# Fourier mixing and MLP layers: the last product with w4 as seven block products, channels by tokens, behind all of w3

## The chip, the core and the metric

The kernel runs on one core of a Trainium2 chip. TensorE multiplies, VectorE (DVE) and ScalarE (ACT) do the elementwise work, GpSimd (POOL) a few small ones, and SyncE (SP) issues every DMA from one queue, in order. The metric is the time of one execution in microseconds on the device. Before the change three executions took 1460.28, 1461.61 and 1462.27 us; the median is 1461.61 us.

## The reference

The input x has 2048 tokens of 512 channels in float32. Two layers A are interleaved with two layers B, each added to its input:

```python
x = x + A(layernorm(x)); x = x + B(layernorm(x)); x = x + A(layernorm(x)); x = x + B(layernorm(x))
def A(x):   # Fourier mixing, real part
    a = x @ dft_hid_re.T; b = x @ dft_hid_im.T
    return dft_seq_re @ a - dft_seq_im @ b
def B(x):   # w1, w2: 512x512, w3: 512x1376, w4: 1376x512
    h = gelu(layernorm(x) @ w1)            # then each quarter of h is shifted by -2..+2 tokens
    x1 = x + shifted(h) @ w2
    return x1 + gelu(layernorm(x1) @ w3) @ w4
```

## The kernel before

Every matrix operand is split into a high and a low part, and `mm3` (L283 to L286) makes each product from three matmuls of a 128x128 stationary block with 512 moving columns: high by high, high by low, low by high. The split of an operand is one ACT cast (the high part) and one DVE subtraction (the low part). The hidden width 1376 is padded to NF = 11 blocks of 128. The tokens are cut into four chunks of 512 (c = 0 to 3), each of four tiles of 128.

**Order.** There is no planner: each engine runs its instructions in the order of the code, and waits where an operand is not ready or a buffer is not yet free. That holds for SP too, so a DMA that waits holds up all DMAs behind it.

**The first layer's B.** `by_pairs` (L766) does w1 and w2 for all four chunks, and then w3 and w4 for chunks 0 and 1 together. w3 is done by seven block products in place of eight (a scheme of Winograd's kind: columns of the two chunks, halves of the channels and pairs of hidden blocks), from sums of w3's blocks that DVE makes, splits, and also stores to DRAM (`w3_sums`, `w3_lows`, `w3_keep`, L882 to L906) for the second layer. w4 is done plainly by `w4_part` (L1012): tokens by channels, 12 matmuls per hidden block and chunk. Chunks 2 and 3 then go one after the other through `mlp` (L712) in STEPS = 13 steps t: step t multiplies w3's block t (12 matmuls, gelu on ACT, split on DVE) and, from t = 2, the hidden block t - 2 by w4 (12 matmuls). `stream` (L272) hands each step its weights from a ring of four buffers: at step t it issues the DVE subtraction for step t + 2's weights (L247), the load of a raw buffer behind it (L212), and the ACT cast of step t + 3's (L230). From step 7 of chunk 2 on, the code after `mlp`'s yield (L1335 to L1353) also puts in the preparation of the second layer's first stage, on DVE and ACT.

**The second layer's B.** `by_pairs` runs two pairs. In each, a loop over p (five of them) does the seven block products for two hidden blocks of both chunks (42 matmuls), and between them two `w4_part`s for the first chunk; the second chunk's gelus are kept in `hc`, and its eleven `w4_part`s follow behind the loop, without a break, as the last work of the kernel. The rows of `out` are stored as tokens by channels.

Of the kernel before, what the change touches and what calls it, by code (L numbers as in the profile page):

```python
# [8 lines left out]
F32 = mybir.dt.float32  # L9
F32R = mybir.dt.float32r  # L10
AF = mybir.ActivationFunctionType
# [29 lines left out]


@with_exitstack
def spectral_mlp_kernel(ctx: ExitStack, tc: tile.TileContext, x, ws, hs, w1, w2, w34, out):
    nc = tc.nc
    const = ctx.enter_context(tc.tile_pool(name="const", bufs=1))
    small = ctx.enter_context(tc.tile_pool(name="small", bufs=4))
# [14 lines left out]
    w3d = [dram.tile([P, 2, 7, 2 * P], F32, name=f"w3d{i}") for i in range(NF // 2)]  # L62
    w3e = dram.tile([P, 2, CH], F32, name="w3e")
    w4d = [dram.tile([P, 2, CH], F32, name=f"w4d{i}") for i in range(NF)]

# [52 lines left out]
    scratch = [at(f"scr{i}", RNG + w * 4 * CH, KD, CH, dtype=F32) for i, w in enumerate((2, 3, 0))]  # L118
    extra = [at(f"extra{i}", EXT + i * D, D, dtype=F32) for i in range(6)]
    rest = [at(f"rest{i}", RAWS + i * D, D, dtype=F32) for i in range(8)]  # L120

    def xt(j):
        return xs[j // 2][:, j % 2]
# [156 lines left out]
        return slots.pop(i)  # L280


    def mm3(o, lh, ll, rh, rl, first, last):  # L283
        nc.tensor.matmul(o, lh, rh, start=first, stop=False)  # L284
        nc.tensor.matmul(o, lh, rl, start=False, stop=False)  # L285
        nc.tensor.matmul(o, ll, rh, start=False, stop=last)  # L286

    def stats(srcs):

# [158 lines left out]
    def add(o, a, b, op=ALU.add):  # L448
        nc.vector.tensor_tensor(o, a, b, op=op)
# [196 lines left out]
    def split_low(dst, g):  # L646
        nc.vector.tensor_tensor(dst[:, 1], g, dst[:, 0].bitcast(F32), op=ALU.subtract)
# [110 lines left out]
    def prod(o, w, u, b):  # L758
        for d in range(2):
            v = slice(d * P, (d + 1) * P)  # L760
            mm3(o, w[:, 0, u, v], w[:, 1, u, v], blk[b][:, d, 0], blk[b][:, d, 1], d == 0, d == 1)

    def rt_in(c):
        nc.sync.dma_start(rtf[c % 2][:, :, 1], z3d[c].rearrange("(d p) t -> p d t", p=P))

    def by_pairs(layer, zs, xin, dst):  # L766
        act = nc.scalar.copy
        w1p = [stream(), stream()]
# [74 lines left out]
        fs = [NF - 1] + list(range(NF - 1))  # L843
        order = [None] + fs + fs
        n_pairs = 1 if layer == 0 else NC // 2
        seq, used = {"n": 0}, {"n": 0}

        def w4_fresh(n):
# [1 line left out]

        def w4_load():
            n = seq["n"]
            if n == n_pairs * len(order):
# [176 lines left out]
        def one():  # L1030
            if bg:
                bg.pop(0)()

        for pair in range(n_pairs):
            c1, c2 = 2 * pair, 2 * pair + 1
            bk, acc1 = (mm4, acc4) if pair == 0 else (acc4, mm4)
            acc2 = [bk[(1 + i) % 4] for i in range(4)]
# [140 lines left out]
    for layer in range(LAYERS):  # L1178
# [153 lines left out]
            break  # L1332

        tmps[:] = singles
        for c in (2, 3):  # L1335
            for t in mlp(c, acc4, mm4):
                if c == 2 and t == 1:
                    rt_in(3)
                if c == 2 and t in (9, 10):
                    rt_split(3, ((2 * t - 18, 2 * t - 16),))  # L1340
                if c == 3 and t == 1:
                    for j in range(2 * TC, 3 * TC, 2):
                        rows(xs[j // 2], x2d, j, 2, False)
# [63 lines left out]
```

## Time and profile before

| what | value |
|---|---|
| median of three executions | 1461.61 us |
| span of the profiled execution, first to last instruction | 1459.5 us |
| median less the span of the profiled execution | 2.1 us |
| TensorE busy | 1450.2 us, 99% of the span |
| DVE, ACT busy | 1123.6 us (77%), 717.9 us (49%) |
| chunks 2 and 3 of the first layer (`mlp`) | from 618.4 us |
| last pair of the second layer | from 1341.4 us |

The profiled execution has no time of its own beside its span; the median above stands for it, 2.1 us longer than the span. In the views, L12 is line 12 of the kernel; names such as psd or w3b are tiles with their numbers left out, "out<-in" tells what an instruction writes and reads, and the text in brackets how long its engine sat idle before it and what ended that. "SPq" is SP's DMA queue; a DMA row gives the issue alone, and "to landing" the time from issue until the data is there. TensorE rows overlap: the time one matmul costs is the distance between two starts, not the duration in the row.

### The profile page before, as it was taken

Reading aid. Unit: us, or ns where it says so; the run is one execution under the profiler, and the core shown is the slowest. Engines: PE = TensorE matmul, PEld = TensorE weight load, DVE = VectorE, ACT = ScalarE, POOL = GpSimd, SP = SyncE. Lnnn points to the kernel's source line nnn. Section 1 sums busy time; section 2 is a strip of 40 time slices with the busy share of each in tenths; the row PEclk is TensorE's granted clock in tenths of the full one; section 3 lists DMA queues with packets and bytes.
Section 4 is the critical chain, followed back from the end, with each engine's and each line's share of the span. In section 5 each row is a group of like instructions: output and inputs, shape, how many; then the busy total and the mean of one; then the engine's idle time right before and its main releaser. Section 6 shows DMA issues by size and latency. Waiting matters only on the chain.

```text
span 1459.5 us, 17324 instructions
## 1 busy us (share of the span) xinstructions
PE 1450.2 (99%) x6374; PEld 1189.0 (81%) x6374; DVE 1123.6 (77%) x1560; ACT 717.9 (49%) x953; POOL 86.4 (6%) x111
## 2 busy tenths in 40 slices
PE   9999999999999999999999999999999999999998
PEld 7888888888878788887887888888887788888887
DVE  7876987988868896658889978979797788646443
ACT  5563454444556664335554543545445575423231
POOL 2100000000001000001100000000000010000000
PEclk9999999999999999999999999999999999999999
DMA  7336556556545767842445555564665466768434
GB/s 251 124 95 209 192 187 212 188 186 235 185 136 169 237 237 278 264 150 86 139 137 195 169 199 204 165 230 173 209 229 168 130 173 260 236 225 295 157 126 159
DMA packets 110500, 277.17 MB, mean 190 GB/s; under 512 B 8400, under 2 KB 37072, under 8 KB 108496
## 3 DMA queue, kind: packets, MB, share of 16 engines
q1 hardware_dynamic: 110416, 276.07, 56.5%
q8 instruction: 50, 0.82, 0.2%
q14 instruction: 34, 0.28, 0.1%
HBM read 231.21 MB, written 44.83 MB: 189 GB/s over the span
## 4 chain that ended last, share of the span: by engine, by line
PE 86%; DVE 8%; DMA 3%; issue 1%; ACT 1%; SPq 0%; POOL 0%; DVEq 0%; ACTq 0%; POOLq 0%
PE psd L284 9%; PE psd L286 9%; PE psd L285 9%; PE psa L284 8%; PE psa L286 7%; PE psa L285 7%; PE psc L286 6%; PE psc L284 6%; PE psc L285 6%; PE psb L286 6%; PE psb L284 6%; PE psb L285 6%; DVE ring L247 2%; DMA raw<-in_ws 2%; DVE ring3f L236 0%
## 5 line engine op out<-in xcount | busy, mean ns | idle before, releaser
L230 ACT CAST ring<-raw 128x1024 fp32r<-128x1024 f32 (+1 forms) x153 | 156.9, 1031 | 122.8 <-PE psd L286 49.3
L247 DVE TENSOR_TENSOR ring<-raw,ring 128x1024 fp32r<-128x1024 f32 (+1 forms) x154 | 182.1, 1186 | 28.6 <-ACT ring L230 28.5
L286 PE MATMUL psd<-ring,rr 128*128 128x512 f32 x208 | 80.9, 389 | 0.0
L285 PE MATMUL psd<-ring,rr 128*128 128x512 f32 x208 | 80.9, 389 | 0.0
L284 PE MATMUL psd<-ring,rr 128*128 128x512 f32 x208 | 80.9, 389 | 0.0
L324 POOL TENSOR_TENSOR rs<-ve,mhalf 128x4 f32<-128x4 f32 x16 | 27.8, 1739 | 612.9 <-DVE nm L323 612.9
L303 POOL TENSOR_TENSOR rs<-ve,mhalf 128x2 f32<-128x2 f32 (+1 forms) x33 | 32.9, 998 | 405.8 <-DVE nb L302 405.8
L332 ACT ACTIVATE tmp<-xs,nb,rs 128x512 f32<-128x512 f32 x58 | 44.7, 810 | 16.3 <-POOL nb L304 16.3
L237 ACT CAST ring<-ring2f 128x1024 fp32r<-128x1024 f32 x28 | 29.6, 1057 | 44.2 <-DVE ring2f L236 44.2
L285 PE MATMUL psc<-ring,ay 128*128 128x512 f32 x128 | 50.0, 391 | 1.0 <-DVE ring L247 1.0
L284 PE MATMUL psc<-ring,ay 128*128 128x512 f32 x128 | 49.9, 390 | 0.3 <-ACT rr11f L474 0.3
L237 ACT CAST ring<-ring0f 128x1024 fp32r<-128x1024 f32 x28 | 29.6, 1058 | 41.5 <-DVE ring0f L236 41.5
L286 PE MATMUL psc<-ring,ay 128*128 128x512 f32 x128 | 49.9, 390 | 0.0
L284 PE MATMUL psb<-ring,ay 128*128 128x512 f32 x128 | 49.8, 389 | 0.0
L285 PE MATMUL psb<-ring,ay 128*128 128x512 f32 x128 | 49.8, 389 | 0.0
L286 PE MATMUL psb<-ring,ay 128*128 128x512 f32 x128 | 49.8, 389 | 0.0
L247 DVE TENSOR_TENSOR ring<-ring1f,ring 128x1024 fp32r<-128x1024 f32 (+1 forms) x50 | 49.2, 984 | 0.6 <-ACT ring L233 0.4
L247 DVE TENSOR_TENSOR ring<-ring3f,ring 128x1024 fp32r<-128x1024 f32 (+1 forms) x50 | 49.2, 984 | 0.2
L284 PE MATMUL psd<-ring,ay 128*128 128x512 f32 x126 | 49.0, 389 | 0.0
L286 PE MATMUL psd<-ring,ay 128*128 128x512 f32 x126 | 49.0, 389 | 0.0
L284 PE MATMUL psa<-ring,ay 128*128 128x512 f32 x126 | 49.0, 389 | 0.0
L285 PE MATMUL psa<-ring,ay 128*128 128x512 f32 x126 | 49.0, 389 | 0.0
(481 smaller groups left out, 4353.4 us busy)
## 6 DMA issues: line engine op xcount, KB each, us to landing
raw<-in_ws SPq DMA_DIRECT2D x183, 512.0 KB, 4.9
raw<-in_hs SPq DMA_DIRECT2D x56, 512.0 KB, 3.5
w4r<-w4d SPq DMA_DIRECT2D x55, 512.0 KB, 3.8
w3b<-w3d SPq DMA_DIRECT2D x10, 1792.0 KB, 7.5
raw<-in_w SPq DMA_DIRECT2D x26, 512.0 KB, 3.7
w3d<-w3b SPq DMA_DIRECT2D x5, 1792.0 KB, 6.7
x1d<-tmp SPq DMA_DIRECT2D x12, 512.0 KB, 6.8
xs<-x1d SPq DMA_DIRECT2D x12, 512.0 KB, 6.7
```

The costliest lines, as they stand in the source:

```text
L230: nc.scalar.copy(dest[:, a:b, 0], r[0][:, a:b])
L237: nc.scalar.copy(dest[:, :, 0], lo)
L247: nc.vector.tensor_tensor(lo[:, i], src[:, i], hi[:, i].bitcast(F32), op=ALU.subtract)
L284: nc.tensor.matmul(o, lh, rh, start=first, stop=False)
L285: nc.tensor.matmul(o, lh, rl, start=False, stop=False)
L286: nc.tensor.matmul(o, ll, rh, start=False, stop=last)
L303: nc.gpsimd.tensor_tensor(rs[:, :n], ve[:, :n], mhalf[:, 0, :n], op=ALU.pow)
L324: nc.gpsimd.tensor_tensor(rs, ve, mhalf[:, :, :2], op=ALU.pow)
L332: nc.scalar.activation(o, s, AF.Identity, bias=mr[2], scale=mr[1])
```

## The change

Only the second layer's last pair (chunks 2 and 3) and the place where its weights come from are changed.

- **Last pair.** `last_pair` does all of w3 first: the leftover block's 24 matmuls, and then five rounds of 42, now with eight PSUM banks in turn. All gelus (22 blocks of 128x512) stay in SBUF, and DVE makes 21 sums of them (t1, t2, t3 in place of b12, t4 in place of b21). Then w4 is done the other way round, channels by tokens: weights are the stationary operand and hidden blocks the moving one. Seven passes of 30 matmuls (five steps of six) do ten hidden blocks; 24 matmuls for the eleventh are spread over passes 0, 1, 3 and 4. Every step's hidden block is split by an ACT cast and a DVE subtraction three steps ahead (`split_of`). The last pass's matmuls are issued only at its end, first all for one bank, then all for the other.
- **Weights.** Each pass loads its five blocks, 1,310,720 bytes in rows of 1 KB, from `w4s` in DRAM into one of two buffers, which lie where w3's two buffers were. The load for pass i + 1 is issued as pass i begins.
- **First layer.** w4's sums and splits are made in steps 0 to 7 of chunk 2's `mlp`, right behind each step's own instructions: `w4_ahead(t)` stores pair t - 2 of hidden blocks to `w4s` (1792 KB), makes pair t - 1's low parts on DVE, makes pair t's sums on DVE (four of 128x256) and its casts on ACT, and loads pair t + 1 (512 KB). The sums of pair t go into the buffer from which pair t - 2 is stored, since there are two.
- **Result.** Chunks 2 and 3 leave as `out_t`, channels by tokens, in their natural order; the residual is transposed in 32x32 blocks on DVE, stored and loaded again. The host turns `out_t` back.

```diff
--- before.py
+++ after.py
...
@@ -62,6 +62,9 @@
     w3d = [dram.tile([P, 2, 7, 2 * P], F32, name=f"w3d{i}") for i in range(NF // 2)]
     w3e = dram.tile([P, 2, CH], F32, name="w3e")
     w4d = [dram.tile([P, 2, CH], F32, name=f"w4d{i}") for i in range(NF)]
+    w4s = dram.tile([P, NF // 2, 2, 7, 2 * P], F32, name="w4s")
+    w4e = dram.tile([P, 2, 4, 2 * P], F32, name="w4e")
+    resd = [dram.tile([D, CH], F32, name=f"resd{i}") for i in range(2)]
...
@@ -118,6 +121,19 @@
     scratch = [at(f"scr{i}", RNG + w * 4 * CH, KD, CH, dtype=F32) for i, w in enumerate((2, 3, 0))]
     extra = [at(f"extra{i}", EXT + i * D, D, dtype=F32) for i in range(6)]
     rest = [at(f"rest{i}", RAWS + i * D, D, dtype=F32) for i in range(8)]
+    w4c, w4cf = zip(*(both(f"w4c{i}", word, 2, 7, 2 * P) for i, word in enumerate((W12, 0))))
+    w4raw = [at(f"w4raw{i}", word, 2, CH, dtype=F32) for i, word in enumerate((STG, EXT, EXT + 2 * CH))]
...
+    h_at = [XS + i * CH for i in range(4)] + [W12 + i * CH for i in range(NF + 4)]
+    h_at += [ZW + i * CH for i in range(8)] + [RR + (8 + i) * CH for i in range(8)]
+    hq = [at(f"hq{i}", word, CH, dtype=F32) for i, word in enumerate(h_at)]
+    hs_at = [XS + 4 * CH, XS + 6 * CH, STG] + [H3 + 2 * i * CH for i in range(4)] + [XS + 12 * CH, XS + 14 * CH]
+    hsplit = [at(f"hs{i}", word, 2, CH) for i, word in enumerate(hs_at)]
+    w4u = [at(f"w4u{i}", RNG + 8 * CH + i * 28 * P, NF // 2, 2, 2 * P) for i in range(2)]
+    w4t = at("w4t", XS + 8 * CH, 2, 4, 2 * P)
...
@@ -763,6 +779,58 @@
     def rt_in(c):
         nc.sync.dma_start(rtf[c % 2][:, :, 1], z3d[c].rearrange("(d p) t -> p d t", p=P))
+    W4_UNITS = {"12": 0, "1": 1, "2": 2, "3": 3, "a11": 4, "a12": 5, "a22": 6}
...
+    def w4_raw(n):
+        to = w4raw[n % 3]
+        if n < NF // 2:
+            nc.sync.dma_start(to, w34[2 * n + LAG : 2 * n + LAG + 2, :, 1].rearrange("f p w -> p f w"))
+        else:
+            nc.sync.dma_start(to[:, 0], w34[NF - 1 + LAG, :, 1])
+    def w4_parts(n):
+        r, lo = w4raw[n % 3].rearrange("p f (e w) -> p f e w", e=2), w4cf[n % 2][:, 1]
+        if n < NF // 2:
+            return [(slice(0, 4), lo[:, 0:4]), (slice(4, 6), r[:, :, 0]), (slice(6, 7), r[:, 1, 1:2])]
+        return [(slice(0, 2), lo[:, 0:2]), (slice(2, 4), r[:, 0])]
+    def w4_sums(n):
+        lo = w4cf[n % 2][:, 1]
+        (a11, a21), (a12, a22) = ([w4raw[n % 3][:, f, e * 2 * P : (e + 1) * 2 * P] for e in range(2)] for f in range(2))
+        if n < NF // 2:
+            add(lo[:, 1], a21, a22)
+            add(lo[:, 3], a11, a21, ALU.subtract)
+            add(lo[:, 2], lo[:, 1], a11, ALU.subtract)
+            add(lo[:, 0], a12, lo[:, 2], ALU.subtract)
+        else:
+            add(lo[:, 0], a11, a21, ALU.subtract)
+            add(lo[:, 1], a21, a11, ALU.subtract)
+        for units, src in reversed(w4_parts(n)):
+            nc.scalar.copy(w4c[n % 2][:, 0, units], src)
+    def w4_lows(n):
+        w = w4c[n % 2]
+        for units, src in reversed(w4_parts(n)):
+            nc.vector.tensor_tensor(w[:, 1, units], src, w[:, 0, units].bitcast(F32), op=ALU.subtract)
+    def w4_keep(n):
+        w = w4c[n % 2].bitcast(F32)
+        if n < NF // 2:
+            nc.sync.dma_start(w4s[:, n], w)
+        else:
+            nc.sync.dma_start(w4e, w[:, :, 0:4])
+    def w4_ahead(t):
+        if 0 <= t - 2 <= NF // 2:
+            w4_keep(t - 2)
+        if 0 <= t - 1 <= NF // 2:
+            w4_lows(t - 1)
+        if 0 <= t <= NF // 2:
+            w4_sums(t)
+        if t + 1 <= NF // 2:
+            w4_raw(t + 1)
...
@@ -850,7 +919,7 @@
         def w4_load():
...
+        def last_pair():
...
+            def split_of(m):
+                key, b = steps[m][2], hsplit[m % len(hsplit)]
+                if key[0] == "t4":
+                    q = key[1]
+                    add(slots["b21", q], slots["t2", q], slots["b21", q], ALU.subtract)
+                    slots[key] = slots["b21", q]
+                nc.scalar.copy(b[:, 0], slots[key])
+                split_low(b, slots[key])
+                splits[m] = b
+            def gelu_to(key, src):
+                nc.scalar.activation(slot(key), src, AF.Gelu_apprx_tanh)
+            def residual(c):
+                return [
+                    *[lambda q=q: [turn_one(turn4, i, xt(c * TC + i)) for i in (q, q + 1)] for q in (0, 2)],
+                    lambda: turn_out(turn4, resd[c - c1]),
+                ]
+            def res_in(i):
...
+            def sums(p):
+                t1 = slot(("t1", p))
+                add(t1, slots["b12", p], slots["b11", p], ALU.subtract)
+                if p < NF // 2:
+                    t2 = slot(("t2", p))
+                    add(t2, slots["b22", p], t1, ALU.subtract)
+                    add(slots["b12", p], slots["b22", p], slots["b12", p], ALU.subtract)
+            todo = residual(c1) + [lambda: None] * 4 + residual(c2)
...
+            def w4_in(i, u):
+                nc.sync.dma_start(w4u[i % 2].bitcast(F32), w4s[:, :, :, W4_UNITS[u]])
+            last = NF // 2
+            passes = [
+                ("a11", "b11", 2), ("2", "t2", 0), ("a12", "b21", None), ("1", "t1", 3),
+                ("3", "b12", 1), ("12", "b22", None), ("a22", "t4", None),
+            ]
+            steps = []
+            for i, (u, h, e) in enumerate(passes):
+                steps += [(i, p, (h, p), None) for p in range(NF // 2)]
+                if e is not None:
+                    steps.append((i, last, ("t1" if h == "t2" else h, last), e))
+            for p in range(NF // 2):
+                u, v, x, y = sets[p % 2]
+                w = w3b[(5 + p) % 2]
+                b1, b6, b5, b2, b7, b4, b3 = (bank() for _ in range(7))
...
+                sums(p - 1 if p else last)
...
+                if p == last - 1:
+                    w4_in(0, passes[0][0])
+                    split_of(0)
+                    split_of(1)
...
+                w3_load(5 + p + 2)
+                if p == 3:
+                    nc.sync.dma_start(w4t.bitcast(F32), w4e)
+            assert not todo
+            w4_in(1, passes[1][0])
+            for i in range(2):
+                res_in(i)
+            c_1, y_12 = part4[:2]
...
+            def give(i, half, src, bk, op=ALU.add, which=(0, 1)):
+                r = resid[i][:, 2 * half : 2 * half + 2]
+                for j in which:
+                    add(r[:, j], src[:, j], bk[j], op)
+                    nc.sync.dma_start(out_v[:, 2 * half + j, i * CH : (i + 1) * CH], r[:, j])
+            def after(i, bk):
+                if i == 0:
+                    for j in range(2):
+                        nc.scalar.copy(c_1[:, j], bk[j])
+                    sums(last - 1)
+                if i == 1:
+                    for j in range(2):
+                        add(c_1[:, j], c_1[:, j], bk[j])
+                if i == 2:
+                    give(0, 0, resid[0][:, 0:2], bk)
+                if i == 3:
+                    for j in range(2):
+                        add(y_12[:, j], c_1[:, j], bk[j])
+                    for half in range(2):
+                        r = resid[1][:, 2 * half : 2 * half + 2]
+                        add(r, r, y_12)
+                if i == 4:
+                    give(1, 1, resid[1][:, 2:4], bk)
+                    for j in range(2):
+                        add(c_1[:, j], c_1[:, j], bk[j])
+                    add(resid[0][:, 2:4], resid[0][:, 2:4], c_1)
+                if i == 5:
+                    give(1, 0, resid[1][:, 0:2], bk)
+            bks, kept = {}, []
+            for k, (i, p, key, e) in enumerate(steps):
+                if k + 3 < len(steps):
+                    split_of(k + 3)
+                first = p == 0
+                if first:
+                    bks[i] = bks[0] if i == 2 else [bank(), bank()]
+                    if 0 < i < len(passes) - 1:
+                        w4_in(i + 1, passes[i + 1][0])
+                w = w4u[i % 2][:, p] if e is None else w4t[:, :, e]
+                h = splits.pop(k)
+                end = k + 1 == len(steps) or steps[k + 1][0] != i
+                if i == len(passes) - 1:
+                    kept.append((w, h))
+                    continue
+                for j in range(2):
+                    v = slice(j * P, (j + 1) * P)
+                    mm3(bks[i][j], w[:, 0, v], w[:, 1, v], h[:, 0], h[:, 1], first and i != 2, end, i == 2)
+                if end:
+                    after(i, bks[i])
+            for j in range(2):
+                v = slice(j * P, (j + 1) * P)
+                for p, (w, h) in enumerate(kept):
+                    mm3(bks[i][j], w[:, 0, v], w[:, 1, v], h[:, 0], h[:, 1], p == 0, p == last - 1)
+                give(0, 1, resid[0][:, 2:4], bks[i], ALU.subtract, (j,))
         for pair in range(n_pairs):
+            if pair:
+                last_pair()
+                break
             c1, c2 = 2 * pair, 2 * pair + 1
             bk, acc1 = (mm4, acc4) if pair == 0 else (acc4, mm4)
             acc2 = [bk[(1 + i) % 4] for i in range(4)]
@@ -1332,8 +1579,11 @@
             break
         tmps[:] = singles
+        w4_raw(0)
         for c in (2, 3):
             for t in mlp(c, acc4, mm4):
+                if c == 2:
+                    w4_ahead(t)
                 if c == 2 and t == 1:
                     rt_in(3)
                 if c == 2 and t in (9, 10):
...
```

More of the change, by code (lines that the diff above doesn't have):

```diff
@@ L43, in spectral_mlp_kernel @@
 @with_exitstack
-def spectral_mlp_kernel(ctx: ExitStack, tc: tile.TileContext, x, ws, hs, w1, w2, w34, out):
+def spectral_mlp_kernel(ctx: ExitStack, tc: tile.TileContext, x, ws, hs, w1, w2, w34, out, out_t):
     nc = tc.nc
@@ L120, in spectral_mlp_kernel @@
     rest = [at(f"rest{i}", RAWS + i * D, D, dtype=F32) for i in range(8)]
+    w4c, w4cf = zip(*(both(f"w4c{i}", word, 2, 7, 2 * P) for i, word in enumerate((W12, 0))))
[7 more added lines that the diff above has]
+    w4t = at("w4t", XS + 8 * CH, 2, 4, 2 * P)
+    resid = [at(f"resid{i}", i * 4 * CH, KD, CH, dtype=F32) for i in range(2)]
+    part4 = [at(f"part{i}", RR + 2 * i * CH, 2, CH, dtype=F32) for i in range(2)]
+    turn4 = at("turn4", RAWS, KD, CH, dtype=F32)
     def xt(j):
@@ L280, in stream, with mm3 @@
         return slots.pop(i)
[L283 to L286, printed above, removed]
+    def mm3(o, lh, ll, rh, rl, first, last, onto=False):
+        nc.tensor.matmul(o, lh, rh, start=first, stop=False, skip_group_check=onto)
+        nc.tensor.matmul(o, lh, rl, start=False, stop=False, skip_group_check=onto)
+        nc.tensor.matmul(o, ll, rh, start=False, stop=last, skip_group_check=onto)
     def stats(srcs):
@@ L845, in by_pairs @@
         n_pairs = 1 if layer == 0 else NC // 2
+        loads = len(order) + (1 if layer else 0)
         seq, used = {"n": 0}, {"n": 0}
@@ L852, in w4_load @@
             n = seq["n"]
-            if n == n_pairs * len(order):
+            if n == loads:
                 return
@@ L1032, in one, with bank, slot, one_more @@
                 bg.pop(0)()
+        def last_pair():
+            c1, c2 = NC - 2, NC - 1
+            n = {"bank": 0, "slot": 0}
+            banks = acc4 + mm4
+            slots, splits = {}, {}
+            def bank():
+                n["bank"] += 1
+                return banks[(n["bank"] - 1) % 8]
+            def slot(key):
+                n["slot"] += 1
+                slots[key] = hq[n["slot"] - 1]
+                return slots[key]
+            def split_of(m):
[15 more added lines that the diff above has]
+            def res_in(i):
+                nc.sync.dma_start(resid[i], resd[i].rearrange("(d p) t -> p d t", p=P))
+            def sums(p):
[6 more added lines that the diff above has]
+            todo = residual(c1) + [lambda: None] * 4 + residual(c2)
+            def one_more():
+                if todo:
+                    todo.pop(0)()
+            s = w4_use()
+            for key, names in (("b11", ("11", "21")), ("b12", ("12", "22"))):
+                o = bank()
+                for d in range(KD):
+                    b = blk[names[d // 2]]
+                    v = slice(d * P, (d + 1) * P)
+                    mm3(o, s[:, 0, v], s[:, 1, v], b[:, d % 2, 0], b[:, d % 2, 1], d == 0, d == KD - 1)
+                gelu_to((key, NF // 2), o)
+                one_more()
+            def w4_in(i, u):
[14 more added lines that the diff above has]
+                b1, b6, b5, b2, b7, b4, b3 = (bank() for _ in range(7))
+                prod(b1, w, 4, "11")
+                nc.scalar.copy(u, b1)
+                one_more()
+                prod(b6, w, 1, "t2")
+                add(v, u, b6)
+                prod(b5, w, 0, "t1")
+                add(x, v, b5)
+                sums(p - 1 if p else last)
+                prod(b2, w, 5, "21")
+                add(u, u, b2)
+                gelu_to(("b11", p), u)
+                prod(b7, w, 2, "t3")
+                add(v, v, b7)
+                add(y, v, b5)
+                gelu_to(("b22", p), y)
+                one_more()
+                if p == last - 1:
+                    w4_in(0, passes[0][0])
+                    split_of(0)
+                    split_of(1)
+                prod(b4, w, 6, "t4")
+                add(v, v, b4)
+                gelu_to(("b21", p), v)
+                if p == last - 1:
+                    split_of(2)
+                prod(b3, w, 3, "22")
+                add(x, x, b3)
+                gelu_to(("b12", p), x)
+                w3_load(5 + p + 2)
[6 more added lines that the diff above has]
+            c_1, y_12 = part4[:2]
+            out_v = out_t.rearrange("(d p) t -> p d t", p=P)
+            def give(i, half, src, bk, op=ALU.add, which=(0, 1)):
[51 more added lines that the diff above has]
+                give(0, 1, resid[0][:, 2:4], bks[i], ALU.subtract, (j,))
@@ L1399 @@
     ]
-    args.append(nc.dram_tensor("out", (S, D), F32, kind="ExternalOutput").ap())
+    args.append(nc.dram_tensor("out", (S // 2, D), F32, kind="ExternalOutput").ap())
+    args.append(nc.dram_tensor("out_t", (D, S // 2), F32, kind="ExternalOutput").ap())
     with tile.TileContext(nc) as tc:
@@ L1404 @@
     out = np.empty((S, D), a["A_x"].dtype)
-    out[at] = r.results[0]["out"]
+    out[at[: S // 2]] = r.results[0]["out"]
+    out[S // 2 :] = r.results[0]["out_t"].T
     return out.reshape(_OUT)
```

## The prediction

> **What bounds the kernel now.** I read the page first, then the windows by stage, then single steps of the timeline, and last the DMA views.
>
> ```profile
> span 1459.5 us, 17324 instructions
> PE 1450.2 (99%) x6374; PEld 1189.0 (81%) x6374; DVE 1123.6 (77%) x1560; ACT 717.9 (49%) x953; POOL 86.4 (6%) x111
> PE 86%; DVE 8%; DMA 3%; issue 1%; ACT 1%; SPq 0%; POOL 0%; DVEq 0%; ACTq 0%; POOLq 0%
> ```
>
> TensorE never stops, and the chain that ended last is 86% TensorE. A matmul removed is therefore time won at its pitch; work added elsewhere is free only until TensorE has to wait for it. Where is there room? The stages that the change touches:
>
> ```profile
> core 0: us, PE busy (x) PEld busy (x) DVE busy (x) ACT busy (x) POOL busy (x), PEclk, DMA share, GB/s
> 618.40:656.50 38.10, 38.10 (x170) 31.54 (x169) 20.12 (x30) 12.00 (x16) 0.00 (x0) 1.00 0.43 153
> 656.50:668.00 11.50, 11.50 (x52) 9.55 (x51) 6.25 (x13) 5.31 (x8) 1.87 (x2) 1.00 0.24 68
> 678.00:690.00 12.00, 11.95 (x52) 9.31 (x50) 11.50 (x22) 7.24 (x11) 1.37 (x2) 1.00 0.26 89
> 690.00:702.00 12.00, 11.39 (x51) 9.36 (x51) 11.69 (x22) 7.66 (x12) 2.16 (x2) 1.00 0.66 218
> 1341.40:1419.50 78.10, 78.10 (x344) 64.17 (x343) 33.22 (x49) 23.49 (x38) 0.00 (x0) 1.00 0.47 159
> 1419.50:1455.70 36.20, 36.20 (x157) 29.07 (x155) 12.24 (x18) 7.03 (x12) 0.00 (x0) 1.00 0.45 148
> ```
>
> The first row is steps 0 to 7 of chunk 2's MLP in the first layer, where w4's preparation goes: DVE is free for 18.0 of 38.1 us. From 678 us on DVE is full, and TensorE already idles there. The last two rows are the last pair.
>
> **Part 1, the matmuls.** Pitch is read from starts:
>
> ```profile
> 1341.37 0.39 PE L284 MATMUL psc<-b,w4r 128*128 128x512 f32 x1
> 1353.61 0.40 PE L284 MATMUL psd<-w4r,h 128*128 128x512 f32 x1
> 1419.48 0.40 PE L284 MATMUL psd<-w4r,h 128*128 128x512 f32 x1
> 1455.34 0.40 PE L286 MATMUL psc<-w4r,h 128*128 128x512 f32 x1
> ```
>
> Between the first two rows lie 54 matmuls of w3 (24 + 5 x 6): 12.24 / 54 = 0.2267 us. The last 156 matmuls of w4 (13 x 12) take (1455.34 - 1419.48) / 155 = 0.2314 us each. Removed are 11 blocks x 4 x 3 x 2 chunks = 264 of these, 61.1 us. Added are 7 x 30 + 24 = 234. Their form is that of w3's products (a block of weights held, 512 tokens moved, two banks), so I take 0.2267: 53.0 us. **Gain 8.1 us**; at 0.2314 it would be 6.9.
>
> **Part 2, the preparation in the first layer.** The code adds per step: three DVE subtractions (256, 512, 1024 wide), four DVE sums of 256, three ACT casts, a load of 512 KB and a store of 1792 KB. Their prices, and the step into which they go:
>
> ```profile
> 688.49 0.42 DVE L365 TENSOR_TENSOR ax2f<-tmp 128x256 f32<-128x256 f32 x1
> 688.83 0.69 DVE L366 TENSOR_TENSOR ay2f<-tmp 128x512 f32<-128x512 f32 x1
> 689.43 1.22 DVE L247 TENSOR_TENSOR ring<-raw,ring 128x1024 fp32r<-128x1024 f32 x1
> 690.56 0.42 DVE L650 CAST h<-tmp 128x512 fp32r<-128x512 f32 x1
> ...
> 619.83 1.57 SPq L203 DMA_DIRECT2D x2d<-xs  x2
> 628.47 1.22 DVE L247 TENSOR_TENSOR ring<-raw,ring 128x1024 fp32r<-128x1024 f32 x1
> 629.49 1.05 ACT L230 CAST ring<-raw 128x1024 fp32r<-128x1024 f32 x1 [2.12 <-PE psa L286]
> 629.75 5.84 SPq L212 DMA_DIRECT2D raw<-in_w  x2
> 632.21 0.60 ACT L644 ACTIVATE tmp<-psb 128x512 f32<-128x512 f32 x1 [1.67 <-PE psb L286]
> 632.84 0.43 DVE L650 CAST h<-tmp 128x512 fp32r<-128x512 f32 x1 [3.15 <-ACT tmp L644]
> 633.37 0.69 DVE L647 TENSOR_TENSOR h<-tmp,h 128x512 fp32r<-128x512 f32 x1
> 633.98 1.22 DVE L247 TENSOR_TENSOR ring<-raw,ring 128x1024 fp32r<-128x1024 f32 x1
> 656.49 0.39 PE L284 MATMUL psc<-rt,ring 128*128 128x512 f32 x1
> ```
>
> By the starts of the first four rows DVE gives a 256-wide operation 0.34 us, 512 wide 0.60, 1024 wide 1.13. A step adds 0.34 + 0.60 + 1.13 + 4 x 0.34 = 3.4 us of DVE; TensorE's step is 24 x 0.2267 = 5.44 us. By volume that fits. But the engines run in order, so what counts is the loop of waits. Call E(t) the end of DVE's last new sum in step t.
>
> Behind E(t) come, in order: ACT's cast of the sums (1.05), its ring cast (1.05) and the gelu (0.60); DVE's cast and subtraction of the hidden block (0.46 + 0.60), the three subtractions (2.07), the four sums (1.4), handoffs some 0.1. That is 7.4 us a step against 5.44.
>
> From step 2 on another loop is longer. The sums of pair t overwrite the buffer from which pair t - 2 is stored, and this store is put into SP's queue only in step t itself, behind the load of a raw buffer. The rows at 628.47 and 629.75 show what that load waits for: it is issued 0.06 us after a ring subtraction ends (628.47 + 1.22 = 629.69), and in the new code the next ring subtraction stands behind E(t - 1). So the store is issued at E(t - 1) + 1.2 + 0.4, and DVE waits until it has landed, with every later hidden block queued behind it. What a store of this size takes:
>
> ```profile
> w3d<-w3b SPq DMA_DIRECT2D x1, 1792.0 KB, 8.4
> DMA to landing us min/median/max: 6.3/6.7/9.4
> staged<-in_w SPq DMA_DIRECT2D x5, 512.0 KB, 3.5
> raw<-in_w SPq DMA_DIRECT2D x12, 512.0 KB, 5.0
> ```
>
> The second row is for all five stores of w3 (L907), the first is the one behind 1 MB of loads. Here 512 KB stand ahead, so I take 7.2, with 6.3 and 9.4 as bounds. A step then takes 1.6 + 7.2 + 1.5 = **10.3 us**.
>
> The times: the first load goes out behind the stores at 619.83 + 1.57 = 621.4 and lands 4 us later (3.5 to 5.0 above); E(0) = 626.9, E(1) = 634.3, then E(2) = 644.6, E(3) = 654.9, E(4) = 665.2, and E(5) = 674.8, with two sums in place of four. TensorE's step 8 needs a ring subtraction that stands behind E(5): it starts at 674.8 + 1.3 = 676.1, where the row above has 656.49. **Loss 19.6 us**; by the bounds of the landing 16 to 28. The ring's three steps of reserve are already spent in this.
>
> What follows is the stretch from 678 us in which DVE is full and which until now is entered with that reserve. I charge 2 us more (0 to 4).
>
> The clock is a question here. TensorE would idle some 5 us in each of four steps. At the end of the kernel the trace has such an idle stretch, its last matmul starting at 1455.34:
>
> ```profile
> 1458.00:1459.00 1.00, 0.00 (x0) 0.00 (x0) 0.00 (x0) 0.00 (x0) 0.00 (x0) 1.00 0.03 10
> 1458.80:1459.50 0.70, 0.00 (x0) 0.00 (x0) 0.00 (x0) 0.00 (x0) 0.00 (x0) 0.64 0.00 0
> ```
>
> Full until 1459.0, 0.64 in the last 0.7 us: the clock falls some 3.3 us after the matmuls end. A 5 us gap can thus lower it. At half speed a step is 10.9 us instead of 5.44, about as long as the loop of 10.3, so it costs little until the loop is over, and then some 3 us. I keep this as a rival.
>
> The Trainium skill ("TensorE: Matmul & The Clock Gate", Part 1: The HAM clock gate) has the same rule: half clock after an idle window of about 3.4 us, full again after a busy one. The trace agrees with the fall; by that rule the first step after the last gap would lose up to 1.7 us.
>
> **Part 3, the last pair's waits.** During w3's rounds (42 x 0.2267 = 9.5 us) DVE has seven PSUM sums, three SBUF sums and two transposes at most, some 12 x 0.65 = 7.8 us, and eight banks in turn; the next w3 load has 9.5 us for 7.5. I cost this at nothing. In the w4 passes I do not.
>
> ```profile
> w4r<-w4d SPq DMA_DIRECT2D x55, 512.0 KB, 3.8
> w3b<-w3d SPq DMA_DIRECT2D x10, 1792.0 KB, 7.5
> q1 hardware_dynamic: 2112, 1.05, 57.4%
> 1428.00:1432.00 4.00, 4.00 (x19) 3.24 (x18) 1.39 (x2) 0.94 (x2) 0.00 (x0) 1.00 1.02 404
> ```
>
> No transfer of before has 1 KB rows. Bounds: the 512-byte rows of a transposed chunk (third row, an 8 us window from 1138 us) moved 1.05 MB in 0.574 x 8 = 4.6 us, 228 GB/s; the 4 KB rows moved 404 / 1.02 = 396. In a line between them by time per row, 1 KB comes to 307 GB/s: 4.3 us for 1.31 MB (3.3 to 5.8), and 2.5 us around it as in the first row (3.8 - 0.524 / 0.396), so 6.8 to land. A pass is 30 or 36 matmuls, 6.8 or 8.2 us, so a load issued as a pass begins is just in time, unless something stands ahead. The third pass's load stands behind 2.1 MB of residual: some 1.0 us late. The fifth's is issued behind two stores that wait for DVE: 1.5 us late.
>
> The Trainium skill ("DMA: Bandwidth & Descriptors", Specifications) puts line rate at rows of 512 B and more. The 228 GB/s beside 396 speak against it; by it these loads would land 1 us sooner, and the sum would be 2 us lower.
>
> The last two passes wait for DVE, with these prices:
>
> ```profile
> L449 DVE TENSOR_TENSOR rest<-rest,psc 128x512 f32<-128x512 f32 x11 | 7.6, 688 | 10.9 <-PE psc L286 10.8
> L647 DVE TENSOR_TENSOR h<-hc,h 128x512 fp32r<-128x512 f32 x11 | 7.5, 691 | 17.1 <-ACT h L650 17.1
> L650 ACT CAST h<-hc 128x512 fp32r<-128x512 f32 x11 | 6.9, 623 | 21.0 <-PE psc L285 15.0 <-PE psa L285 6.0
> ```
>
> When the fifth pass ends, DVE has four PSUM sums and one of 1024 (3.9 us), two splits (1.2), three t4 splits, each a DVE sum, an ACT cast and a DVE subtraction one after the other (0.61 + 0.62 + 0.61 + 0.1 = 1.95; 5.8), two output sums (1.4) and two t4 splits (3.9): 16.2 us. TensorE then still has 18 matmuls (4.1): 20.3 against 60 x 0.2267 = 13.6, so 6.7 late. Together **9.2 us of waits**; 3 if the t4 splits overlap, 13.5 with the slowest loads. The tail (one sum, one 256 KB store) stays.
>
> **Sum.** -8.1 + 19.6 + 2 + 9.2 = +22.7 on the span of 1459.5. The median is 2.1 us above that span, and I add the change to the median: 1461.6 + 22.7 = **1484.3 us**.
>
> **Rivals.**
> *It gets faster.* If the stores land before DVE comes to the sums and DVE's free 18.0 us take the preparation within the ring's reserve, TensorE does not wait in the first layer. It decides at E(5): up to 655.2 nothing is lost. With 3 us of waits in the last pair: 1461.6 - 8.1 + 3 = 1456.5. For it: the volume. Against it: five steps in a chain of at least 7.4 us.
> *The store does not bind*, only the handoffs do: E(5) = 634.3 + 3 x 7.4 + 6.7 = 663.2, step 8 at 664.5, 8.0 late, 1 behind it: 1461.6 - 8.1 + 9 + 9.2 = 1471.7.
> *The last pair hides more*: 3 us of waits, with the first layer's loss: 1478.1.
> *The clock falls* in the gaps: 3 more, 1487.3.
> *The gains just meet the losses* within 0.2%: some of each of the above.
>
> **Chances.** Forecast 0.56; store not binding 0.12; last pair hidden 0.10; clock 0.10; faster 0.08; even 0.04. A difference of 0.2% (2.9 us) is about what a measurement of this kernel can tell from none. Faster 0.08, the same 0.04, slower 0.88. The range holds the forecast with its bounds (16 of landing, 3 of waits: 1461.6 - 8.1 + 16 + 3 = 1472.5; upward 1494 with a landing of 9), the clock, and the handoffs alone at 1471.7 with a smaller wait: 1465 to 1495.
>
> **What the profile after would show.** In the first layer, DVE's 256-wide sums waiting for a DMA some 10 us apart, and TensorE idle before ring or h operands, 4 to 5 us in each of steps 5 to 8; step 8 near 676. In the last pair, pitch 0.2267 throughout w4, a gap ahead of the third and fifth pass, gaps in the last two behind DVE. A sum of steps 5.44 us apart, or a store issued before the ring subtraction, would make me wrong in the first layer; a last pass without gaps in the last.

## The result, and the profile after

The changed kernel takes 1493.59 us (median of 4 runs, 1492.61 to 1494.4), the kernel before 1461.76 in the same comparison (4 runs, 1460.28 to 1462.27): a ratio of 1.0217, with a 95% interval of 1.0202 to 1.0231. It is slower, as forecast. On the profiled spans it is 31.2 us slower (1490.7 against 1459.5); the sum had +22.7. The median lies 9.3 us above the forecast of 1484.3 and 1.4 below the upper bound of the range.

The page of the kernel after: its span, the engines' busy time, and the shares of the chain that ended last.

```profile
span 1490.7 us, 17426 instructions
PE 1457.1 (98%) x6344; PEld 1188.8 (80%) x6344; DVE 1177.4 (79%) x1654; ACT 736.3 (49%) x989; POOL 87.2 (6%) x111
PE 83%; DVE 9%; DMA 5%; ACT 2%; issue 1%; SPq 0%; POOL 0%; DVEq 0%; ACTq 0%; POOLq 0%
```

TensorE has its 30 matmuls fewer, and the chain passes from TensorE to DVE and DMA. Where? The timeline of TensorE gives the two stages. First the kernel before: chunk 2's MLP begins at the first row, and the work behind chunk 3's MLP at the second.

```profile
618.41 0.39 PE L284 MATMUL psc<-rt,ring 128*128 128x512 f32 x1
...
739.35 0.39 PE L284 MATMUL psc<-ring,ax 128*128 128x512 f32 x1
```

The same two points of the kernel after, then the last pair's first matmul and its last:

```profile
618.30 0.39 PE L300 MATMUL psc<-rt,ring 128*128 128x512 f32 x1
...
768.89 0.39 PE L300 MATMUL psc<-ring,ax 128*128 128x512 f32 x1
...
1370.03 0.39 PE L300 MATMUL psc<-b,w4r 128*128 128x512 f32 x1
1486.63 0.39 PE L302 MATMUL psc<-hs,w4u 128*128 128x512 f32 x1
```

The two MLPs took 120.9 us and take 150.6: **29.7 us more**. The last pair, from the first rows of its kind to the last matmul's start, took 114.0 (1341.37 to 1455.34) and takes 116.6: **2.6 more**, with fewer matmuls. What lies between became 0.9 us shorter (602.0 before, 601.1 after), which I have not followed. So nearly the whole loss is in the preparation of w4 in the first layer.

The stages of the kernel after, in windows that answer to those of before. Columns are the window, its length, then busy time and count of PE, PEld, DVE, ACT, POOL, then granted clock, DMA share, GB/s:

```profile
core 0: us, PE busy (x) PEld busy (x) DVE busy (x) ACT busy (x) POOL busy (x), PEclk, DMA share, GB/s
618.30:668.00 49.70, 38.90 (x145) 29.29 (x144) 27.17 (x46) 14.25 (x21) 0.00 (x0) 0.90 0.74 258
682.00:686.00 4.00, 4.00 (x11) 3.15 (x12) 2.28 (x4) 3.49 (x6) 0.00 (x0) 0.57 0.77 274
1370.00:1423.70 53.70, 53.24 (x235) 43.77 (x234) 36.96 (x58) 16.04 (x27) 0.00 (x0) 1.00 0.64 206
1423.70:1486.90 63.20, 58.02 (x234) 44.31 (x234) 42.40 (x65) 24.17 (x42) 0.00 (x0) 0.97 0.57 187
```

In the first row TensorE is busy for 38.9 of 49.7 us, where it was busy throughout; and DVE, at 27.2 of 49.7, isn't full either. That is a chain of waits and not a lack of room. What waits for what is in DVE's timeline (the bracket is its idle time before the instruction, and what ended it):

```profile
627.38 0.76 DVE L465 TENSOR_TENSOR w4c0f<-w4raw 128x256 f32<-128x256 f32 x2 [4.38 <-DMA w4raw<-in_w]
...
642.95 1.23 DVE L814 TENSOR_TENSOR w4c<-w4c1f,w4c 128x1024 fp32r<-128x1024 f32 x1
647.15 0.76 DVE L465 TENSOR_TENSOR w4c0f<-w4raw 128x256 f32<-128x256 f32 x2 [2.98 <-DMA w4s<-w4c]
...
648.63 1.22 DVE L263 TENSOR_TENSOR ring<-raw,ring 128x1024 fp32r<-128x1024 f32 x1
...
658.57 0.76 DVE L465 TENSOR_TENSOR w4c1f<-w4raw 128x256 f32<-128x256 f32 x2 [2.92 <-DMA w4s<-w4c]
...
669.82 0.76 DVE L465 TENSOR_TENSOR w4c0f<-w4raw 128x256 f32<-128x256 f32 x2 [2.77 <-DMA w4s<-w4c]
...
680.05 0.76 DVE L465 TENSOR_TENSOR w4c1f<-w4raw 128x256 f32<-128x256 f32 x2 [1.74 <-DMA w4s<-w4c]
```

From 647 us on, the sums of each pair wait for the store of the pair two before (w4s<-w4c), 11.4, 11.3 and 10.2 us apart, and the ring subtraction stands behind them. TensorE's timeline shows the price of one such step:

```profile
644.66 0.39 PE L301 MATMUL psc<-rt,ring 128*128 128x512 f32 x1
649.90 0.80 PE L302 MATMUL psc<-rt,ring 128*128 128x512 f32 x1 [4.85 <-DVE ring L263]
```

### The profile page after: what moved, and what is told of

It is laid out like the page before. It is cut to its first block, busy times and chain, and to the rows that moved or that the text cites. A ratio compares the mean times of both kernels' runs of the same rounds, so it can differ in the third digit from the quotient of the medians.

```text
span 1490.7 us, 17426 instructions
## 1 busy us (share of the span) xinstructions
PE 1457.1 (98%) x6344; PEld 1188.8 (80%) x6344; DVE 1177.4 (79%) x1654; ACT 736.3 (49%) x989; POOL 87.2 (6%) x111
## 4 chain that ended last, share of the span: by engine, by line
PE 83%; DVE 9%; DMA 5%; ACT 2%; issue 1%; SPq 0%; POOL 0%; DVEq 0%; ACTq 0%; POOLq 0%
PE psd L300 9%; PE psd L301 9%; PE psd L302 9%; PE psa L300 8%; PE psa L301 7%; PE psa L302 7%; PE psc L302 6%; PE psc L300 6%; PE psc L301 6%; PE psb L302 5%; PE psb L300 5%; PE psb L301 5%; DMA w4s<-w4c 2%; DVE ring L263 2%; DMA raw<-in_ws 1%
```

## The experiments

The theory is the prediction's: a loop of waits in the first layer (store issued late, landed late, handoffs in order) and DVE's chain in the last passes. The rivals: DVE's volume, the matmuls' pitch, the loads.

**1. The first layer's part alone.** The kernel before, with the new work of the first layer added (the functions as in the changed kernel; here only their calls) and the old last pair:

```diff
...
+        w4_raw(0)
         for c in (2, 3):
             for t in mlp(c, acc4, mm4):
+                if c == 2:
+                    w4_ahead(t)
```

> The kernel before, with w4's sums, splits and stores put into the first layer as in the changed kernel, and the last pair left as it was (what is stored is not read). The theory that the first layer's loss is 28.7 us of the changed kernel's 31.2: 1461.8 + 28.7 = 1490.4 us, with step 8 of the MLP starting 26 to 27 us late. A rival, that the preparation and the last pair disturb each other through DRAM or DMA: under 1485.

Measured: 1491.46 us (1490.07 to 1492.96), ratio 1.0206 (1.0189 to 1.0223); the two MLPs take 151.2 us, the last pair is as before. So the preparation costs 30 us by itself, without a product of the new kind in the kernel, and the last pair's new form costs little.

**2. The store issued earlier.** Each pair is put into the queue right behind its low halves, a step sooner:

```diff
-        if 0 <= t - 2 <= NF // 2:
-            w4_keep(t - 2)
         if 0 <= t - 1 <= NF // 2:
             w4_lows(t - 1)
+            w4_keep(t - 1)
```

> The changed kernel with each store put one step earlier, ahead of the new sums (pair t - 1 is stored in step t). If the wait for the store sets the steps: 8.4 us a step in place of 11.4, E(5) at 670, step 8 at 671 in place of 682, 1493.6 - 11.5 = 1482 us. If the handoffs between DVE and ACT set the steps and the wait for the store only fills time that is lost anyway: unchanged within 2 us of 1493.6.

Measured: 1485.91 us (1485.0 to 1486.87), ratio 1.0164 (1.0149 to 1.018); the MLPs take 143.1, 7.5 less. No sum waits for a store any more. Of the 11.5 us expected 7.7 came: the first sums start 1.8 us later in this execution (629.18 against 627.38), and a new wait costs 1.7 in two steps (0.3 and 1.4). DVE's timeline of this kernel shows the longer one:

```profile
656.16 0.76 DVE L465 TENSOR_TENSOR w4c1f<-w4raw 128x256 f32<-128x256 f32 x2 [1.39 <-DMA w4raw<-in_w]
```

The sums now wait for their own load, which stands behind the store in SP's queue. With the store's lateness taken away the MLPs still take 22.2 us more than before the change, where the rival "the store does not bind" had 9: the handoffs and a load are left. This kernel also shows how stores land with a load behind them. SP's timeline, and the five stores with their median landing time:

```profile
637.71 0.34 SPq L819 DMA_DIRECT2D w4s<-w4c  x1
638.10 0.43 SPq L787 DMA_DIRECT2D w4raw<-in_w  x1
```
```profile
w4s<-w4c SPq DMA_DIRECT2D x5, 1792.0 KB, 6.8
```

**3. The handoffs.** ACT's two casts of the sums are moved a step back, so that no engine waits for them in the step in which the sums are made:

```diff
+    def w4_highs(n):
         for units, src in reversed(w4_parts(n)):
...
         if 0 <= t - 1 <= NF // 2:
+            w4_highs(t - 1)
             w4_lows(t - 1)
```

> The changed kernel with ACT's casts of pair t put into step t + 1, behind its gelu, so that the gelu no longer stands behind DVE's sums; the stores stay. If the wait for the store sets the steps: steps of 11.3 us stay from step 2 on, only the first one is shorter, 1491 us. If the handoffs set them: steps fall to some 6 us, 1478 or less.

Measured: 1492.05 us (1488.88 to 1492.35), ratio 1.0201 (1.0186 to 1.0217), which overlaps with the 1.0202 to 1.0231 of the changed kernel; the MLPs take 148.0. DVE's timeline says why so little came of it:

```profile
646.45 0.76 DVE L465 TENSOR_TENSOR w4c0f<-w4raw 128x256 f32<-128x256 f32 x2 [6.57 <-DMA w4s<-w4c]
...
658.11 0.76 DVE L465 TENSOR_TENSOR w4c1f<-w4raw 128x256 f32<-128x256 f32 x2 [5.64 <-DMA w4s<-w4c]
```

DVE comes sooner and waits longer, 6.57 us where it was 2.98: as long as the store binds, the handoffs are off the path.

**4. Both, and a third buffer.** To 2 and 3 a third buffer of sums is added, so that a store has one step more to land:

```diff
...
-    w4c, w4cf = zip(*(both(f"w4c{i}", word, 2, 7, 2 * P) for i, word in enumerate((W12, 0))))
+    w4c, w4cf = zip(*(both(f"w4c{i}", word, 2, 7, 2 * P) for i, word in enumerate((W12, 0, ZW))))
...
```

> The changed kernel with stores one step earlier, casts one step later, and a third buffer for the sums and splits, so that no sum waits for a store. If waits are all of the loss: a step is bound by TensorE's 5.44 or DVE's 5.8 us, the first layer loses 1 to 3 us, 1493.6 - 25 = 1468 us. If DVE's volume alone costs (3.4 us a step on 2.3): 10 us or more stay lost, 1477 or more.

Measured: 1477.9 us (1476.04 to 1479.38), ratio 1.0109 (1.0094 to 1.0124); the MLPs take 134.9. It looked like the volume theory's number, but the queue's and DVE's timelines show a wait:

```profile
634.12 0.34 SPq L821 DMA_DIRECT2D w4s<-w4c  x1
634.51 0.43 SPq L787 DMA_DIRECT2D w4raw<-in_w  x1
```
```profile
643.17 0.76 DVE L465 TENSOR_TENSOR w4c2f<-w4raw 128x256 f32<-128x256 f32 x2 [3.25 <-DMA w4raw<-in_w]
...
652.96 0.76 DVE L465 TENSOR_TENSOR w4c0f<-w4raw 128x256 f32<-128x256 f32 x2 [3.77 <-DMA w4raw<-in_w]
```

SP puts the load of the next pair into the queue only after the store's wait for DVE, and 1.8 MB of store moves beside it.

**5. The load ahead of the store.** In the kernel of 4, the next pair's load becomes the first call of the step:

```diff
+        if t + 1 <= NF // 2:
+            w4_raw(t + 1)
         if 0 <= t - 1 <= NF // 2:
...
-        if t + 1 <= NF // 2:
-            w4_raw(t + 1)
```

> As the run with the third buffer, earlier stores and later casts, with each load of 512 KB put ahead of the store in SP's queue. In that run DVE's sums wait 3.3 and 3.8 us for these loads. If that is what is left of the loss: chunks 2 and 3 take 128 us in place of 134.9 (120.9 before the change), 1471 us. If DVE's volume holds the steps: unchanged, 1478.

Measured: 1471.15 us (1469.15 to 1473.14), ratio 1.0071 (1.0057 to 1.0085); the MLPs take 129.1. Of 29.7 us lost, 21.5 have been taken back without one instruction less: waits and not volume made at least these.

**6. The last pair's DVE chain.** In the kernel after, the sums t4 are made while the fourth product runs, where DVE has room, and the first three splits come sooner (two of them by two rounds of w3, the third by one):

```diff
-                if key[0] == "t4":
-                    q = key[1]
-                    add(slots["b21", q], slots["t2", q], slots["b21", q], ALU.subtract)
-                    slots[key] = slots["b21", q]
...
+                if p == 2:
                     split_of(0)
                     split_of(1)
...
-                if p == last - 1:
+                if p == 3:
                     split_of(2)
...
+                if i == 3 and p < last:
+                    add(slots["b21", p], slots["t2", p], slots["b21", p], ALU.subtract)
+                    slots["t4", p] = slots["b21", p]
```

> The changed kernel with two things moved in the last pair alone: the five t4 sums into the fourth pass (their inputs are there by then), and the first three splits into w3's rounds 2 and 3. If the waits there are DVE's chain behind the fifth pass and the late first splits: w4's passes take 55 us in place of 63.8, 1493.6 - 8.7 = 1485 us. If the weights' loads in rows of 1 KB stand behind them and come to light once the splits are ready: 60 us or more, 1490.

Measured: 1485.22 us (1485.06 to 1486.83), ratio 1.0171 (1.0156 to 1.0187). The seven products take 54.53 us from the first matmul's start to the last one's end (its start and one pitch of 0.2267), where they took 63.15 (1423.71 to 1486.86) after the change. The window of them in this kernel:

```profile
1424.80:1479.40 54.60, 53.48 (x234) 43.76 (x234) 39.69 (x62) 23.30 (x40) 0.00 (x0) 1.00 0.66 217
```

DVE is nearly as busy in it (39.7 us) as after the change (42.4), and the time is 8.6 us less: the order of DVE's work was the price here.

**7. The t4 sums alone** tell which of the two did it (the last hunk of 6 and the one that takes the sums out, without the splits):

> The changed kernel with the five t4 sums alone moved into the fourth pass. If the forecast's chain behind the fifth pass is most of the waits in w4's passes: 63.2 us from w4's first to its last matmul fall by 6.7 to 56.5 (to 54.5 with the first splits moved too). If the late first splits are most of it: 60 or more.

Measured, in one run: 1487.19 us beside 1460.78 before; the products take 56.65 us. So 6.5 of the 8.6 us are t4's chain, 2.1 the first splits.

**8. All of it together.** 5 and 6 in one kernel, and the first pair's load issued ahead of chunk 2:

```diff
+            if layer == 0:
+                w4_raw(0)
             split_later(2)
...
-        w4_raw(0)
```

> All of these together, and the first load of w4's raw weights issued while the pair before still multiplies, so that the first sums don't wait for it. If the parts are independent: chunks 2 and 3 take 125 us, w4's passes 55, and 1461.7 + 4 + 1 - 6 = 1460 to 1462 us: the gain of 30 matmuls just pays for the rest. If DVE is full from the first step to 700 us into the run, so that work moved earlier only meets the next full stretch: 1465 or more.

Measured: 1459.11 us (11 runs, 1456.05 to 1460.85) beside 1460.83 (21 runs), ratio 0.9985 (0.9977 to 0.9994). The MLPs take 125.8 us, the products 54.53. All parts of the change are in this kernel, and it stands within 0.2% of the kernel before.

**9. Is the rest DVE's volume?** In steps 0 to 7 the hidden block's cast goes from DVE to ACT:

```diff
-                gelu_split(h3[t % (LAG + 1)], ps)
+                gelu_split(h3[t % (LAG + 1)], ps, nc.scalar.copy if c == 2 and t < 8 else nc.vector.tensor_copy)
```

> As the run before, with the cast of the hidden block on ACT in place of DVE in steps 0 to 7 of chunk 2 (0.46 us of DVE a step for 0.62 of ACT). If DVE's volume is what holds these steps at the end: 2 to 3 us less than the run before. If the handoffs still do: the same or up to 2 us more, since ACT's cast stands ahead of the others.

Measured: 1459.19 us (11 runs, 1457.19 to 1460.6), ratio 0.9988 (0.9979 to 0.9997). The MLPs take 2.0 us less, as volume would have it, the products 1.0 more, and the median is the same. Each of these stage times is read from one execution, and those of the kernel of 8 spread over 4.8 us: inconclusive.

**10. The last pair's loads.** The waits in the kernel of 8's last pair leave two for a load of w4:

```profile
PE psa L300 <- DMA w4u<-w4s: 1.1, 1, 1.1
PE psd L300 <- DMA w4u<-w4s: 0.8, 1, 0.8
```

So, in the kernel of 9, the load for product i + 2 is put ahead of the output stores that wait for DVE, as soon as its buffer is free, and the leftover weights two rounds earlier:

```diff
-                if p == 3:
+                if p == 1:
                     nc.sync.dma_start(w4t.bitcast(F32), w4e)
...
-                    if 0 < i < len(passes) - 1:
-                        w4_in(i + 1, passes[i + 1][0])
...
                 if end:
+                    if i + 2 < len(passes):
+                        w4_in(i + 2, passes[i + 2][0])
                     after(i, bks[i])
```

> The run with everything moved and ACT's cast, with two loads of the last pair put ahead: each pass's weights before the output stores in SP's queue, and the eleventh block's weights two rounds earlier. In the run with everything moved TensorE waited 0.9 us for the first pass's weights and 1.3 for the last's. If these loads are late only for what stands ahead of them: 2 us less than 1459.2, 1457. If rows of 1 KB make them late: the same.

Measured: 1456.88 us (7 runs, 1455.02 to 1458.77) beside 1460.78 (17 runs), ratio 0.9974 (0.9963 to 0.9984). This is the lowest median, and its interval excludes a ratio of 1; it overlaps with the intervals of 8 and 9. Two windows, the first layer's steps and the products:

```profile
618.00:702.00 84.00, 80.23 (x348) 64.76 (x347) 72.35 (x127) 50.83 (x75) 7.43 (x8) 1.00 0.76 279
1396.80:1449.90 53.10, 53.10 (x236) 43.99 (x235) 41.65 (x65) 24.57 (x42) 0.00 (x0) 1.00 0.68 222
```

TensorE has no gap left in the products, which take 53.05 us, 234 matmuls at 0.2267. In the first layer it still idles 3.8 of 84 us (0.7 before the change); the MLPs take 125.0 us against 120.9 before.

**11. The sums on GpSimd.** To take those 4 us, w4's sums go from DVE to the idle GpSimd:

```diff
-            add(lo[:, 1], a21, a22)
+            nc.gpsimd.tensor_tensor(lo[:, 1], a21, a22, op=ALU.add)
...
```

> The run before with w4's 22 sums of 128x256 on GpSimd in place of DVE, 1.44 us of DVE a step less. If DVE's volume is the rest of the first layer's loss (2.8 us there): 2 us less, 1455. If GpSimd's sums are slow and ACT's casts wait for them: 1457 or more.

Measured: 1457.43 us (11 runs, 1456.27 to 1459.53), ratio 0.9979 (0.997 to 0.9988), the MLPs 126.8: no gain. The timelines of GpSimd and DVE show one reason. Each pair of rows is one operation, first while the other engine is at work too, then while that one is idle:

```profile
629.99 1.71 POOL L803 TENSOR_TENSOR w4c1f<-w4c1f,w4raw 128x256 f32<-128x256 f32 x1
645.55 0.73 POOL L803 TENSOR_TENSOR w4c0f<-w4c0f,w4raw 128x256 f32<-128x256 f32 x1
...
631.03 1.76 DVE L263 TENSOR_TENSOR ring<-raw,ring 128x1024 fp32r<-128x1024 f32 x1
638.55 1.22 DVE L263 TENSOR_TENSOR ring<-raw,ring 128x1024 fp32r<-128x1024 f32 x1
```

A sum takes 0.42 us on DVE and 0.73 on GpSimd while DVE is idle, but up to 1.71 beside DVE's work, and DVE's own subtraction then takes 1.76 in place of 1.22. So the move gives back a part of what it saves. The other reason is in the waits from 618 to 702 us: ACT's casts wait 13.7 us in all for GpSimd's sums, and DVE then 6.2 for these casts. That DVE's volume makes the last 4 us is thus argued (72 of 84 us busy in 10, above) and not shown: DVE had less work in 9 and in 11, and neither was faster as a whole.

## Why the prediction was right, and where its sizes were off

The direction and the mechanism held: the loss lies where it was put, with the store as the wait that ends last and then DVE's chain in the last products. The sum was 8.5 us short on the span: 5.5 in the first layer up to step 8, 1.6 in the clock, 0.9 in the stretch behind it and 1.5 in the last pair, less the 0.9 us that lie between.

**Matmuls, -8.1.** Right. The last window above has the new products at 0.2267 once nothing else holds them, and 61.1 - 53.05 is 8.1. That part of the change is worth what it was priced at.

**First layer up to step 8, 19.6: it was 25.1.** TensorE's timeline of the kernel after, at step 8:

```profile
679.23 0.39 PE L301 MATMUL psc<-rt,ring 128*128 128x512 f32 x1
682.00 0.63 PE L302 MATMUL psc<-rt,ring 128*128 128x512 f32 x1 [2.38 <-DVE ring L263]
682.42 0.63 PE L300 MATMUL psc<-rt,ring 128*128 128x512 f32 x1
...
688.72 0.39 PE L300 MATMUL psc<-rt,ring 128*128 128x512 f32 x1
```

The third matmul of the step, the first that needs the ring's low half, starts at 682.0; before, it was 0.45 behind 656.49. The forecast was 676.1. TensorE's idle stretches in steps 5 to 8 were 4.9, 3.3, 3.9 and 2.4 us, where 4 to 5 were forecast. The steps, by the ends of the last new sums, each read as the start of the instruction behind it (628.9, 637.2, 648.6, 660.0, 671.3, 680.7 for E(0) to E(5), in place of 626.9, 634.3, 644.6, 654.9, 665.2, 674.8):

- The first sums were 2.0 us late, at 627.38 above: the load of the first pair, issued at 621.14, took 6.2 us to land and not the 4 that I took.
- "That is 7.4 us a step" is 8.4 in the first step (628.9 to 637.2). The sum left out ACT's cast of the blocks that are read straight from the load. It waited for DVE's sums and stood ahead of the others with 0.93 us; ACT's timeline, two steps on:

```profile
648.75 0.92 ACT L809 CAST w4c<-w4raw 128x256 fp32r<-128x256 f32 x2 [7.95 <-DVE w4c0f L465]
649.70 1.04 ACT L809 CAST w4c<-w4c0f 128x1024 fp32r<-128x1024 f32 x1
```

- "So I take 7.2" for the landing of the store is the term that was mis-sized most. The answer for the stores' line in the kernel after:

```profile
DMA to landing us min/median/max: 7.0/8.1/8.2
```

A step was 11.4 = 1.7 + 8.2 + 1.5: from 637.23 to the issue at 638.91, the landing, and the sums until 648.63. Three steps of 11.4, 11.4 and 11.3 stand for 10.3: 3.2 us. The bounds of 6.3 to 9.4 held the landing. ACT's cast is not in this loop, since the store doesn't wait for it. SP's timeline shows what stood around the store:

```profile
638.51 0.34 SPq L228 DMA_DIRECT2D raw<-in_w  x1
638.91 0.42 SPq L819 DMA_DIRECT2D w4s<-w4c  x1
639.42 0.38 SPq L787 DMA_DIRECT2D w4raw<-in_w  x1
```

The load ahead of the store was in the sum, at 0.5 us (7.2 against 6.7), and the one behind it was not. The runs speak for the one ahead as the one that was priced too low. In experiment 2 the 512 KB load stands 0.4 us behind the store; the two such stores with no other transfer issued in the 5 us before them landed in 6.8 and 7.1 us. In the kernel after, the first three stores, with 512 KB some 0.4 us ahead and 512 or 256 KB behind, took 8.1 to 8.2, and the fourth (672.95), with 256 KB ahead and nothing close behind, 7.0. So 512 KB close ahead cost some 1.1 to 1.4 us in place of 0.5. Two stores don't settle it: the second of experiment 2 took 8.9, with 3.9 MB issued in the 8.3 us before it, and the fifth of the kernel after, for which no sum waits, 7.8 with 256 KB ahead. No run takes the load ahead away alone.

Experiments 2 to 5 show that the loop itself was the cause, and that it has three links which take each other's place: the store, then the load behind the store, then the handoffs.

**The clock.** The rival had it fall, and it did: after the last gap 8 matmuls go 0.43 us apart (682.00 to 685.41), with a granted clock of 0.57 from 682 to 686 in the windows above. That costs 8 x 0.2 = 1.6 us, in step 8; in the steps before, the slow matmuls lie inside the loop of 11.4 us. The sum left this out and the rival had 3. From the window of some 3.4 us in the Trainium skill ("TensorE: Matmul & The Clock Gate", Part 1: The HAM clock gate) the estimate was up to 1.7 us in the first step after the last gap, and the trace agrees with this size; the last gap itself, 2.4 us, was shorter than that window.

**The stretch in which DVE is full, 2:** step 9 is 26.8 us late (688.72 against 661.93), the end of the MLPs 29.7, so it was 2.9, within the bounds of 0 to 4.

**Last pair's waits, 9.2.** They were 10.7: 0.6 in the w3 rounds (53.68 us to 1423.71, for 234 matmuls of 0.2267 in 53.05) and 10.1 in the products (63.15). That the size nearly held was in part luck, for the parts did not:

- The start of the products has no term in the sum ("I cost this at nothing" is said of w3's rounds, in the last of which the first splits are made). It took 2.1 us by experiments 6 and 7, from first splits that are ready too late.
- The loads, 2.5 in the sum, ended 0.5 us of TensorE's waits, by the first load and not the third or fifth (it lies in the 0.6 of the w3 rounds). They landed in 6.6 us where 6.8 had been estimated. From the rule of the Trainium skill on rows of 512 B ("DMA: Bandwidth & Descriptors", Specifications) the estimate would have been some 5.8; the measurement is on the side of the slower rows. Only with DVE's sums moved did the loads hold TensorE inside the products: 1.5 us, the difference between 8 and 10 (54.53 and 53.05).
- The t4 chain, 6.7, measured 6.5 (7), but some 1.4 of this was a fall of the clock, which the sum had not put there: from 1482.20 to 1484.33 five matmuls go 0.43 us apart, and the one before took 0.59. The waits of the kernel after, from 1423 to 1491 us (total, times, longest), have ACT behind DVE and TensorE behind ACT, as the prediction had them:

```profile
ACT hs L1125 <- DVE hq L465: 16.8, 5, 9.9
PE psa L300 <- ACT hs L1125: 3.8, 4, 1.8
PE psd L300 <- DMA w4u<-w4s: 0.5, 1, 0.5
```

The granted clock in the last product, in the columns of the windows above, is 0.66:

```profile
1480.00:1483.00 3.00, 2.41 (x6) 1.44 (x5) 0.92 (x3) 0.62 (x1) 0.00 (x0) 0.66 0.00 0
```

**The rivals.** "It gets faster" had 1456.5, if stores land before DVE comes and nothing waits for long. This kernel does not do that; the same work in another order does (10: 1456.88). The volume that spoke for it was real, and the chain that spoke against it decided. "A sum of steps 5.44 us apart" would have shown the prediction wrong; the steps were 8.4 to 11.4. Two sums of the prediction come out a little otherwise, and neither decides anything: the line between the two row rates gives 301 GB/s and 4.4 us for rows of 1 KB, not 307 and 4.3, and a landing of 9 us by itself gives 1491.5, not 1494.

## What to carry to other kernels

A stage with free volume on an engine can still lose when new work makes a loop through several in-order engines: write down the loop (wait, issue, landing, cast, handoff), and compare its length with the step, ahead of any sum of volumes. In a double buffer, issue the store right behind its last producer and the next load ahead of the store; when one link is taken out, look which link binds next, since here two fixes alone were worth 7.7 us and 1.5 (the second not clear of noise), and with a third buffer and the load ahead of the store they were worth 22. Where the last stage of a kernel is short of DVE, make its sums in a stage that is not.

## What the runs showed of the hardware

- TensorE ran the first two of a product's three matmuls before the low half of the ring existed (679.23 and then 682.00 above): a late low half delays only the third.
- Half the clock has a price of 0.43 against 0.2267 us a matmul, and it held for some 3.4 us (682.00 to 685.41) behind a 2.4 us gap that followed other gaps; I had expected it after gaps of 5 us. A first gap of 1.8 us (ahead of 638.51) left the pitch at 0.23.
- A load of 512 KB issued 0.4 us ahead of a store of 1792 KB made it land in 8.1 to 8.2 us; two stores with such a load 0.4 us behind and nothing close ahead landed in 6.8 and 7.1 (experiment 2).
- GpSimd's sum of 128 x 256 took 0.73 us while DVE was idle and up to 1.71 beside DVE's work, and DVE's 1024-wide subtraction 1.76 us in place of 1.22 (experiment 11). What the two share is not shown by these runs.
